# A fused attention and mixer kernel on one core: the sixth key/value chunk, the weight conversions and six channel pieces get other places in the order

## The chip, the cores and the metric

The kernel runs on one core of a Trainium2 chip. The metric is the device time of one execution in microseconds (us). The core has a matrix engine (TensorE, PE in the rows), three engines for elementwise work (VectorE or DVE, ScalarE or ACT, GpSimd or POOL) and a queue that issues transfers (SyncE, SP). Each of them works through its own list of instructions in order; semaphores tie the lists together.

## The reference

Three layers follow one another, for 4 batches of 576 positions.

- Attention with 8 heads of width 64: q and k are rotated, `softmax(q k^T / 8) v` is taken per head, and the heads are laid side by side into `x` of 512 features.
- A channel mix: `xk = mu_k*x + (1-mu_k)*x_prev` and `xr` likewise with `mu_r`, where `x_prev` is `x` moved by one position; then `v = relu(xk @ w_k)^2 @ w_v` (1024 hidden features) and `r = sigmoid(xr @ w_r)`; the output is `r * v`.
- A token and channel mixer: `u = x + (relu(x^T @ w_tok1) @ w_tok2)^T`, and `u + relu(u @ w_ch1) @ w_ch2` with 1536 hidden channels.

The weights arrive as 64-bit floats and are converted on the chip; each operand of a product is split into a high and a low part, and three products (high by high, high by low, low by high) stand for one.

## The kernel before, in words

**Attention.** The heads are worked in 16 pairs of 9 steps, 144 steps in all. A step (`a_step`, from L640) computes a tile of scores (`S_products`, L437, six matmuls into a tile of the pool `S_p`), its row maximum on DVE (L448), the exponential on ACT (L461), the sum's reciprocal on DVE (L471, L473), a high half on ACT (L78, tile `p`) and a low half on DVE (L484). Two or three transposing transfers (L565, L567) then bring the halves into the layout of the second product, `emit_pv` (L580), whose result DVE scales into `x` (`out`, L584 to L586; the rows show the helper's line L85). The last pair's last `out` is the last output of attention. `S_p` has three score tiles of two PSUM banks each, `pv_p` and `acc_p` have one bank each: eight banks in all.

**Keys and values.** `kvr_gen` (from L716) walks over eight chunks, two of 288 positions per batch, numbered 0 to 7; the sixth chunk is n = 5. Each has 4 pieces of interpolated input (`lerp_slice`), 8 blocks `kp` of 12 matmuls (L704 to L706), whose results ACT evicts twice (L769 the relu, L773 its square), and 4 blocks `vp` of 24 matmuls, which ACT evicts at L76 (`vt`). `a_step` advances this generator three times per step at a lower priority than its own work, so that the blocks fall between the score tiles. What is left after the last step is run by the loop `while not kv.done` (L994). A block takes its accumulator from `accps` (L708): the single bank of `acc_p`, or, once `second` is set (L918, after all steps), three times out of four a tile of `S_p`. All of the sixth chunk's blocks are emitted inside the steps, so they share the one bank.

**Conversions.** `Conv` (L179) turns pieces of the 64-bit weights into split parts in four stages, two pieces per `step`: stage 0 loads (L203, SP), stage 1 rescales the high words on ACT (L211), stage 2 merges the words on DVE (L218, L219, L221, and L226 for a row maximum of channel weights), stage 3 writes the high part on ACT (L76 or L78) and the low part on DVE (L107 or L239). `conv1` (L942) holds `w_r` (4 pieces), `w_tok1` (5), `w_tok2` (2) and the first six pieces of `w_ch2`; three of its steps are emitted before the loop at L994 and one with each turn of it. `conv2` (L1014) holds eight pieces of `w_ch1`, `conv3` the rest.

**Gates and tokens.** `gate_gen` (L943) makes four pieces `xs` of `xr` for each half of a batch (ACT L78, DVE L958, ACT L76, POOL L107), in a pool of four buffers that the keys also used, and then four blocks `rp` of 12 matmuls. `tok_gen` (L882 to L912) is the token mixer. Both are interleaved by a loop that also steps `conv2`; the channel mixer `ch_gen` (L1124 to L1128, `c1p` and `co`) follows with `conv3`.

**What sets the order.** A tile scheduler traces the whole program, simulates it, and lists the instructions per engine by readiness and by a priority that grows in the order of emission; `ahead(n)` moves instructions forward by n. `order` and `behind` add an edge that the simulated order must respect, without a semaphore between engines. A tile is given a buffer when one is free in that order.

Of the kernel before, what the change touches and what calls it, by code (L numbers as in the profile page):

```python
# [8 lines left out]
F32R = mybir.dt.float32r  # L9
# [3 lines left out]
ALU = mybir.AluOpType  # L13
# [3 lines left out]
B, H, S, D = 4, 8, 576, 64  # L17
NP = H // 2
QW = 640
HS = 288  # L20
# [8 lines left out]

PV_AT = {7: 0, 12: 1}  # L30

UNIT = [(0, 256), (256, 320)]

KVN, WARM = 5, (22, 4, 4)

CW, HALF, TWICE = DCH // 2, KC // 2, 3

PACE, STEP, REST = (24, 28), 1, 8

RAW, LOW = 3, "P"  # L40

# [26 lines left out]
def body(tc, kin, qin, vw, tabs, ident, mu, w_k, w_v, w_r, w_t1, w_t2, w_c1, w_c2, out):  # L68
# [18 lines left out]
    class ahead:  # L87

        def __init__(self, n):
            self.n = n  # L90
# [19 lines left out]
    with ctx:  # L110
# [11 lines left out]
        P = {}  # L122
# [51 lines left out]
        def behind(o, name):  # L174

            if name in last:
                order(o, last[name])

        class Conv:  # L179


            def __init__(self, cv, weights, name, load=None, low="P", room=None, after=None):
                self.cv, self.name, self.load, self.low, self.room, self.after = cv, name, load, low, room, after
                self.q = [(w, i) for w in weights for i in range(len(w.srcs))]
                if weights[-1].raw:
                    self.q[:0] = [None] * (len(self.q) % 2)
                self.n, self.words, self.t = 0, {}, {}
# [4 lines left out]
            def stage(self, j, i):  # L192
                if not 0 <= i < len(self.q) or self.q[i] is None:
                    return
                weights, k = self.q[i]
                src = weights.srcs[k]
                w = src.shape[1]
                wide = src.dtype == I64
                if j == 0:
                    raw = self.words[i] = weights.words(k)  # L200
                    if self.load:
                        behind(pool.memset(raw[:, 0:1], 0), self.load)
                    sp.dma_start(raw if wide else raw[:, :w], src.bitcast(I32))  # L203
                    return
                if j < 3:
                    hl = self.words[i].rearrange("p (a b) -> p a b", b=2)
                    lw, hw = hl[:, :, 0], hl[:, :, 1]
                if j == 1:
                    v = self.t[i] = self.cv()[:, :w]
                    x = hw if wide else self.words[i][:, :w]  # L210
                    o = act.activation(out=v.bitcast(F32), in_=x.bitcast(F32), func=AF.Copy,  # L211
                                       scale=REBIAS if wide else 1.0)
                    if self.after:
                        behind(o, self.after)
                elif j == 2 and wide:
                    v = self.t[i]
                    m = self.room()[:, :w] if self.room else v
                    yield lambda: dve.tensor_scalar(out=m, in0=v, scalar1=3, scalar2=None, op0=ALU.logical_shift_left)  # L218
                    yield lambda: dve.scalar_tensor_tensor(out=m, in0=hw, scalar=SIGN, in1=m, op0=ALU.bitwise_and,  # L219
                                                           op1=ALU.bitwise_or)  # L220
                    yield lambda: dve.scalar_tensor_tensor(out=v, in0=lw, scalar=29, in1=m,  # L221
                                                           op0=ALU.logical_shift_right, op1=ALU.bitwise_or)
                    if weights.raw:
                        rows, c = weights.rows
                        o = c + k if weights.cut == 1 else 2 * KD + k
                        yield lambda: dve.tensor_reduce(out=rows[:, 0, o:o + 1], in_=v.bitcast(F32),  # L226
                                                        op=ALU.max, axis=AX.X, apply_absolute_value=True)
                elif j == 3 and weights.raw:
                    rows, c = weights.rows
                    o = c + k // weights.cut  # L230
                    if i % 2 == 0 and weights.cut == 2:
                        dve.tensor_tensor(rows[:, 0, o:o + 1], rows[:, 0, 2 * KD + k:2 * KD + k + 1],
                                          rows[:, 0, 2 * KD + k + 1:2 * KD + k + 2], op=ALU.max)
                        p2(rows[:, :, o:o + 1])
                    elif i % 2 == 0:
                        p2(rows[:, :, o:o + 2])
                    dst, f = weights.take(k), self.t.pop(i).bitcast(F32)
                    copy("A", dst[:, 0], f, rows[:, 1, o:o + 1])
                    yield lambda: dve.scalar_tensor_tensor(out=dst[:, 1], in0=f, scalar=rows[:, 1, o:o + 1],  # L239
                                                           in1=dst[:, 0], op0=ALU.mult, op1=ALU.subtract)  # L240
                elif j == 3:
                    dst, f = weights.take(k), self.t.pop(i).bitcast(F32)
                    copy("A", dst[:, 0], f)
                    tt(self.low, dst[:, 1], f, dst[:, 0].bitcast(F32), ALU.subtract)
# [324 lines left out]
        @prio("pv")  # L569
        def emit_pv(g, u):  # L570

            t0, n = UNIT[u]
            ts = [pt_t.pop((g, x, u)) for x in range(2)]
            vh, vl = v16_t[g]
            p = pv_p.tile([128, 512], F32, tag="pv", name="pv")
            prods = [(vh, j, j) for j in range(9)] + [(vl, j, j) for j in range(5)]
            for i, (v, a, c) in enumerate(prods):
                for x in (1, 0):
                    l = slice(64 * x, 64 * x + 64)
                    pe.matmul(p[l, 0:n], lhsT=v[:, a, l], rhs=ts[x][:, c, :], start=(i == 0),  # L580
                              stop=(i == len(prods) - 1))

            @prio("low")
            def out():  # L584
                b, pr = divmod(g, NP)
                copy("D", x_of(b)[:, pr, 1 + t0:1 + t0 + n], p[:, 0:n], sc_t[g][:, 1:2])  # L586
                if u == 1:
                    x_done(g)
            return out
# [117 lines left out]

        def accps(nm):  # L708
            n_acc[0] += 1
            if second and n_acc[0] % 4:  # L710
                return S_p.tile([128, 2, 512], F32, tag="S", name=nm)[:, 0]
            return acc_p.tile([128, 512], F32, tag="acc", name=nm)

# [2 lines left out]
        def kvr_gen(seq, ready):  # L716
# [28 lines left out]
            for n, (kind, b, c) in enumerate(seq):  # L745
# [4 lines left out]
                if len(xs_of[n]) < KD:  # L750
                    if not xs_of[n]:
                        yield 0
                    while len(xs_of[n]) < KD:
                        lerp(n)
                        tick()
                        yield 0
                xs = xs_of[n]
                k2 = [None] * KF
                for m in range(KF):
# [98 lines left out]
            return s[1] * NP in a_done  # L858

        kv = Stream(kvr_gen([("K", b, c) for b in range(B) for c in range(2)], ready))  # L860
        second = False
        u_of, u_done, M = {}, set(), {}
        for j in range(FIRST, NTT + 5):
            a_step(j, kv.advance)
        at.close()

# [72 lines left out]
        def cv_t():  # L939
            return cv_p.tile([128, S], I32, tag="cv", name="cv")  # L940

        cv = Conv(cv_t, [wr, t1, t2, c2_part(0, HALF)], "conv1", low="D")  # L942
        def gate_gen(b):  # L943

            y = y_p[b].tile([128, KD, S], F32, tag="y", name="y")
# [3 lines left out]
            for c in range(2):  # L949
# [4 lines left out]
                for kk in range(KD):  # L954
                    a = P["a"].tile([128, HS], F32, tag="a", name="a")
                    copy("A", a, x[:, kk, o:o + HS], om_s[:, 1, kk:kk + 1])
                    f = P["f"].tile([128, HS], F32, tag="f", name="f")
                    dve.scalar_tensor_tensor(out=f, in0=x[:, kk, o + 1:o + HS + 1], scalar=mu_s[:, 1, kk:kk + 1], in1=a,  # L958
                                             op0=ALU.mult, op1=ALU.add)
                    t = P["xs"].tile([128, 2, HS], F32R, tag="xs", name="xs")  # L960
                    copy("A", t[:, 0], f)
                    tt("P", t[:, 1], f, t[:, 0].bitcast(F32), ALU.subtract)
                    xs.append(t)
                    yield 2
# [24 lines left out]

        g_done, g_up = set(), []  # L990
        gate, tok = Stream(gates()), Stream(toks())
        for _ in range(3):
            cv.step()
        while not kv.done:  # L994
            kv.advance(30)
            if len(half) == 2 * B and not g_up:
                gate.advance(9)
                g_up.append(1)
            if not cv.done():
                cv.step()  # L1000
# [10 lines left out]
        c2_b = c2_part(HALF, KC)  # L1011
        for nm, n in (("ytk", 1), ("h1", 2), ("uhl", 2), ("hs", 3), ("ht", 2), ("st", 2), ("top", 1)):
            M[nm] = top("m_" + nm, n)
        cv, cv3 = Conv(cv_t, c1_w[:1], "conv2", low="D"), Conv(cv_t, [c1_w[1], c2_b], "conv3", low="D", after="hs")  # L1014
        def all_max(m):

            p = tps("mp")
# [231 lines left out]
```

## Time and profile before

| | us |
|---|---|
| median of 3 runs | 924.8 |
| lowest and highest | 923.28, 929.65 |
| the profiled execution's own time | 928.29 |
| its span, first to last instruction | 926.5 |
| PE busy in the span | 869.4 |

The profile is one execution. Its span is 1.8 us shorter than its own time, which is 3.5 us over the median. Engines are busy at the same time, so their busy times don't add up to the span; for each stage one asks which engine has no room left, and what an idle engine was waiting for.

### The profile page before, as it was taken

The page shows a single profiled execution, that of the slowest core. Times are in us where ns is not written, and L with a number is a line of the kernel's source. Part 1 is how long each engine was busy: PE and PEld are TensorE (multiplying, and loading weights), DVE is VectorE, ACT ScalarE, POOL GpSimd, SP SyncE. Part 2 cuts the span into 40 slices and gives each one's busy share as a digit, 9 for nine tenths or more (in the row PEclk, how much of TensorE's full clock was granted, in tenths as well). Part 3 has the DMA queues.
Part 4 walks back from the last instruction along what each step waited for, and adds up shares of the span by engine and source line. Part 5 has one row for each costly group of instructions (what it writes and reads, how often), then busy time and mean ns, then how long its engine had stood idle before and what let it go on. Part 6 is the DMA issues. An engine that isn't in the chain of part 4 may idle for free.

```text
span 926.5 us, 19002 instructions
## 1 busy us (share of the span) xinstructions
PE 869.4 (94%) x7004; PEld 762.4 (82%) x7004; DVE 620.2 (67%) x1462; ACT 516.9 (56%) x1158; POOL 459.1 (50%) x512
## 2 busy tenths in 40 slices
PE   8899779989989989998899899999999999999998
PEld 5788668889878868897799799998878888888876
DVE  5789877676776757877998745455889445546332
ACT  4798677666876756966655555544456422323221
POOL 6998968776776682623633355422123222222221
PEclk9999979999999989998999999999999999999999
DMA  8786599999999969999836520001220001000000
GB/s 236 255 308 188 134 207 187 209 192 195 204 206 183 221 143 176 153 201 237 289 116 208 151 96 8 2 1 35 75 92 24 1 1 52 27 27 27 27 27 26
DMA packets 172493, 119.17 MB, mean 129 GB/s; under 512 B 133488, under 2 KB 148976, under 8 KB 171888
## 3 DMA queue, kind: packets, MB, share of 16 engines
q1 hardware_dynamic: 172400, 117.95, 52.9%
q8 instruction: 55, 0.90, 0.4%
q14 instruction: 38, 0.31, 0.1%
HBM read 60.90 MB, written 14.16 MB: 81 GB/s over the span
## 4 chain that ended last, share of the span: by engine, by line
PE 43%; DVE 6%; DMA 2%; ACT 2%; issue 2%; POOL 1%; SPq 0%; DVEq 0%; ACTq 0%; POOLq 0%
PE co L704 5%; PE c1p L704 5%; PE c1p L705 5%; PE c1p L706 5%; PE co L705 5%; PE co L706 5%; PE rp L705 2%; PE rp L704 2%; PE rp L706 2%; DVE cv L219 1%; DVE cv L221 1%; PE t2p L911 1%; PE t2p L912 1%; PE t2p L910 1%; PE trp L882 1%
## 5 line engine op out<-in xcount | busy, mean ns | idle before, releaser
L107 POOL TENSOR_TENSOR hs<-ht,hs 128x288 f16<-128x288 f32 x96 | 73.3, 764 | 229.6 <-DVE ht L1128 115.6
L437 PE MATMUL S<-kz,kq 128*128 128x288 f32 x744 | 127.5, 309 | 12.3 <-DVE p L484 3.4
L1124 ACT ACTIVATE hs<-c1p,top 128x288 f16<-128x288 f32 x96 | 47.7, 497 | 161.7 <-PE c1p L706 160.2
L448 DVE TENSOR_REDUCE nm<-S 128x1 f32<-128x576 f32 x144 | 107.9, 753 | 34.0 <-PE S L437 33.2
L437 PEld LDWEIGHTS S<-kz,kq 128*128 128x128 f32 x744 | 107.1, 193 | 23.3 <-issue 14.7
L705 PE MATMUL c1p<-uhl,parts 128*128 128x288 f16 x384 | 109.8, 286 | 0.0
L706 PE MATMUL c1p<-uhl,parts 128*128 128x288 f16 x384 | 109.7, 286 | 0.0
L704 PE MATMUL c1p<-uhl,parts 128*128 128x288 f16 x384 | 109.5, 286 | 0.0
L705 PE MATMUL co<-hs,parts 128*128 128x288 f16 x384 | 108.7, 286 | 0.0
L706 PE MATMUL co<-hs,parts 128*128 128x288 f16 x384 | 108.6, 286 | 0.0
L704 PE MATMUL co<-hs,parts 128*128 128x288 f16 x384 | 105.1, 286 | 0.3 <-ACT hs L1124 0.3
L484 DVE SCALAR_TENSOR_TENSOR p<-S,rc,p 128x576 f16<-128x576 f32 x108 | 85.9, 812 | 17.9 <-ACT p L78 17.3
L461 ACT ACTIVATE S<-S,nm 128x576 f32<-128x576 f32 x108 | 76.9, 715 | 36.5 <-DVE nm L448 36.1
L704 PEld LDWEIGHTS <-parts 128*128 128x128 f16 x768 | 75.1, 98 | 19.3 <-issue 0.5
L705 PEld LDWEIGHTS <-parts 128*128 128x128 f16 x768 | 75.2, 98 | 18.8
L706 PEld LDWEIGHTS <-parts 128*128 128x128 f16 x768 | 75.2, 98 | 18.5
L704 PE MATMUL kp<-xs,parts 128*128 128x288 f32 x256 | 79.4, 313 | 9.9 <-ACT t L769 6.9
L107 POOL TENSOR_TENSOR q<-t 128x288 f32<-128x288 f32 x64 | 45.5, 713 | 80.7 <-ACT t L769 70.7
L78 ACT ACTIVATE p<-S,rc 128x576 f16<-128x576 f32 x108 | 79.0, 754 | 10.6 <-DVE rc L473 6.2
L1128 DVE TENSOR_SCALAR ht<-c1p,top 128x288 f32<-128x288 f32 x60 | 30.9, 516 | 77.7 <-ACT hs L1124 77.7
L704 PE MATMUL vp<-k,parts 128*128 128x288 f32 x256 | 76.0, 301 | 3.5 <-ACT vt L76 1.9
L705 PE MATMUL kp<-xs,parts 128*128 128x288 f32 x256 | 77.7, 304 | 0.2 <-POOL xs L107 0.2
(154 smaller groups left out, 2392.7 us busy)
## 6 DMA issues: line engine op xcount, KB each, us to landing
rq<-in_qin_dram SPq DMA_DIRECT2D x30, 320.0 KB, 4.1
kz<-kq SPq DMA_DIRECT2D x64, 144.0 KB, 2.9
rk<-in_kin_dram SPq DMA_DIRECT2D x30, 288.0 KB, 3.8
words<-in_w_c_dram SPq DMA_DIRECT2D x12, 512.0 KB, 4.2
words<-in_w_c_dram SPq DMA_DIRECT2D x16, 384.0 KB, 3.5
vr<-in_vw_dram SPq DMA_DIRECT2D x16, 320.0 KB, 3.5
xd<-xT SPq DMA_DIRECT2D x16, 288.5 KB, 3.3
xT<-xd SPq DMA_DIRECT2D x4, 1154.0 KB, 5.8
```

The source lines that it names most:

```text
L78: act.activation(out=o, in_=i, func=AF.Copy, scale=scale)
L107: return (pool if e == "P" else dve).tensor_tensor(o, a, b, op=op)
L219: yield lambda: dve.scalar_tensor_tensor(out=m, in0=hw, scalar=SIGN, in1=m, op0=ALU.bitwise_and, op1=ALU.bitwise_or)
L437: o = pe.matmul(p[:, h, 0:HS], lhsT=a[l, 128 * m:128 * m + 128], rhs=b[l, h * HS:(h + 1) * HS], start=(n == 0), stop=(n == 2))
L448: last["max"] = dve.tensor_reduce(out=nm, in_=S_t[j][:, :, 0:HS], op=ALU.max, axis=AX.XY, negate=True)
L461: act.activation(out=e, in_=e, func=AF.Exp, bias=sum_t[j], accum_out=s)
L484: last["lo"] = dve.scalar_tensor_tensor(out=t[:, 1], in0=S_t.pop(j)[:, :, 0:HS], scalar=sum_t[j], in1=t[:, 0], op0=ALU.mult, op1=ALU.subtract)
L704: pe.matmul(p, lhsT=wh, rhs=t[:, 0], start=first, stop=False)
L705: pe.matmul(p, lhsT=wh, rhs=t[:, 1], start=False, stop=False)
L706: pe.matmul(p, lhsT=wl, rhs=t[:, 0], start=False, stop=last)
L1124: last["hs"] = act.activation(out=h[:, 0], in_=p[:, 0:HS], func=AF.Relu, scale=g)
L1128: dve.tensor_scalar(out=f, in0=p[:, 0:HS], scalar1=g, scalar2=0.0, op0=ALU.mult, op1=ALU.max)
```

## The change

Five edits.

- The sixth chunk (`HELD = 5`) is not started until the flag `wide` is set, at the last but one of the 144 steps (`LATE = 2`). A step emits the score tile of two steps later, so by then the program has emitted them all.
- From then on `accps` may take tiles of `S_p`: the test is `wide`, no longer `second`.
- Stage 1 and the first instruction of stage 2 of `conv1` are ordered behind `last["out"]`, the last output of attention; `out` names the instruction for this. The eviction itself is the same instruction as before.
- `conv1` is stepped twice ahead of the loop, no longer three times, and the loop advances the keys by 60, no longer by 30, per step of the conversions. The six pieces of `w_ch2` move from `conv1` to the end of `conv2`.
- The pieces `xs` of the second half (c = 1) of each batch take their buffers from the pool `uhl`, which the channel mixer uses later.

```diff
--- before.py
+++ after.py
@@ -29,13 +29,15 @@
 
 PV_AT = {7: 0, 12: 1}
 
+HELD, LATE = 5, 2
+
 UNIT = [(0, 256), (256, 320)]
 
 KVN, WARM = 5, (22, 4, 4)
 
 CW, HALF, TWICE = DCH // 2, KC // 2, 3
 
-PACE, STEP, REST = (24, 28), 1, 8
+PACE, STEP, REST, SPREAD = (24, 28), 1, 8, 60
 
 RAW, LOW = 3, "P"
 
@@ -179,8 +181,8 @@
         class Conv:
 
 
-            def __init__(self, cv, weights, name, load=None, low="P", room=None, after=None):
-                self.cv, self.name, self.load, self.low, self.room, self.after = cv, name, load, low, room, after
+            def __init__(self, cv, weights, name, load=None, low="P", room=None, after=None, then=None):
+                self.cv, self.name, self.load, self.low, self.room, self.after, self.then = cv, name, load, low, room, after, then
                 self.q = [(w, i) for w in weights for i in range(len(w.srcs))]
                 if weights[-1].raw:
                     self.q[:0] = [None] * (len(self.q) % 2)
@@ -210,12 +212,15 @@
                     x = hw if wide else self.words[i][:, :w]
                     o = act.activation(out=v.bitcast(F32), in_=x.bitcast(F32), func=AF.Copy,
                                        scale=REBIAS if wide else 1.0)
-                    if self.after:
-                        behind(o, self.after)
+                    for x in (self.after, self.then):
+                        behind(o, x)
                 elif j == 2 and wide:
                     v = self.t[i]
                     m = self.room()[:, :w] if self.room else v
-                    yield lambda: dve.tensor_scalar(out=m, in0=v, scalar1=3, scalar2=None, op0=ALU.logical_shift_left)
+                    o = dve.tensor_scalar(out=m, in0=v, scalar1=3, scalar2=None, op0=ALU.logical_shift_left)
+                    if self.then:
+                        behind(o, self.then)
+                    yield
                     yield lambda: dve.scalar_tensor_tensor(out=m, in0=hw, scalar=SIGN, in1=m, op0=ALU.bitwise_and,
                                                            op1=ALU.bitwise_or)
                     yield lambda: dve.scalar_tensor_tensor(out=v, in0=lw, scalar=29, in1=m,
@@ -583,7 +588,8 @@
             @prio("low")
             def out():
                 b, pr = divmod(g, NP)
-                copy("D", x_of(b)[:, pr, 1 + t0:1 + t0 + n], p[:, 0:n], sc_t[g][:, 1:2])
+                last["out"] = dve.tensor_scalar(out=x_of(b)[:, pr, 1 + t0:1 + t0 + n], in0=p[:, 0:n],
+                                                scalar1=sc_t[g][:, 1:2], scalar2=None, op0=ALU.mult)
                 if u == 1:
                     x_done(g)
             return out
@@ -707,7 +713,7 @@
 
         def accps(nm):
             n_acc[0] += 1
-            if second and n_acc[0] % 4:
+            if wide and n_acc[0] % 4:
                 return S_p.tile([128, 2, 512], F32, tag="S", name=nm)[:, 0]
             return acc_p.tile([128, 512], F32, tag="acc", name=nm)
 
@@ -754,6 +760,9 @@
                         lerp(n)
                         tick()
                         yield 0
+                while n == HELD and not wide:
+                    tick()
+                    yield 0
                 xs = xs_of[n]
                 k2 = [None] * KF
                 for m in range(KF):
@@ -858,9 +867,10 @@
             return s[1] * NP in a_done
 
         kv = Stream(kvr_gen([("K", b, c) for b in range(B) for c in range(2)], ready))
-        second = False
+        second = wide = False
         u_of, u_done, M = {}, set(), {}
         for j in range(FIRST, NTT + 5):
+            wide = j >= NTT - LATE
             a_step(j, kv.advance)
         at.close()
 
@@ -939,7 +949,8 @@
         def cv_t():
             return cv_p.tile([128, S], I32, tag="cv", name="cv")
 
-        cv = Conv(cv_t, [wr, t1, t2, c2_part(0, HALF)], "conv1", low="D")
+        c2_a = c2_part(0, HALF)
+        cv = Conv(cv_t, [wr, t1, t2], "conv1", low="D", then="out")
         def gate_gen(b):
 
             y = y_p[b].tile([128, KD, S], F32, tag="y", name="y")
@@ -957,7 +968,12 @@
                     f = P["f"].tile([128, HS], F32, tag="f", name="f")
                     dve.scalar_tensor_tensor(out=f, in0=x[:, kk, o + 1:o + HS + 1], scalar=mu_s[:, 1, kk:kk + 1], in1=a,
                                              op0=ALU.mult, op1=ALU.add)
-                    t = P["xs"].tile([128, 2, HS], F32R, tag="xs", name="xs")
+                    if c == 0:
+                        t = P["xs"].tile([128, 2, HS], F32R, tag="xs", name="xs")
+                    else:
+                        if kk % 2 == 0:
+                            two = M["uhl"].tile([128, 2, 2, HS], F32R, tag="uhl", name="xs")
+                        t = two[:, kk % 2]
                     copy("A", t[:, 0], f)
                     tt("P", t[:, 1], f, t[:, 0].bitcast(F32), ALU.subtract)
                     xs.append(t)
@@ -989,10 +1005,10 @@
 
         g_done, g_up = set(), []
         gate, tok = Stream(gates()), Stream(toks())
-        for _ in range(3):
+        for _ in range(2):
             cv.step()
         while not kv.done:
-            kv.advance(30)
+            kv.advance(SPREAD)
             if len(half) == 2 * B and not g_up:
                 gate.advance(9)
                 g_up.append(1)
@@ -1011,7 +1027,7 @@
         c2_b = c2_part(HALF, KC)
         for nm, n in (("ytk", 1), ("h1", 2), ("uhl", 2), ("hs", 3), ("ht", 2), ("st", 2), ("top", 1)):
             M[nm] = top("m_" + nm, n)
-        cv, cv3 = Conv(cv_t, c1_w[:1], "conv2", low="D"), Conv(cv_t, [c1_w[1], c2_b], "conv3", low="D", after="hs")
+        cv, cv3 = Conv(cv_t, [c1_w[0], c2_a], "conv2", low="D"), Conv(cv_t, [c1_w[1], c2_b], "conv3", low="D", after="hs")
         def all_max(m):
 
             p = tps("mp")
```

## Rows read from the trace of the kernel before

**Rows 1.** The page, busy time and share of the span of each engine.
```profile
PE 869.4 (94%) x7004; PEld 762.4 (82%) x7004; DVE 620.2 (67%) x1462; ACT 516.9 (56%) x1158; POOL 459.1 (50%) x512
```
**Rows 2.** Busy time by stretch; the first of the rows names the columns.
```profile
core 0: us, PE busy (x) PEld busy (x) DVE busy (x) ACT busy (x) POOL busy (x), PEclk, DMA share, GB/s
361.70:413.20 51.50, 49.47 (x414) 46.20 (x413) 39.53 (x95) 38.76 (x88) 21.99 (x29) 1.00 0.93 179
413.20:429.40 16.20, 16.10 (x146) 15.12 (x145) 11.37 (x26) 10.40 (x24) 4.39 (x6) 1.00 0.99 196
...
432.40:442.70 10.30, 8.58 (x34) 7.54 (x32) 10.02 (x18) 6.19 (x14) 4.54 (x6) 0.50 1.00 194
...
477.50:516.50 39.00, 38.37 (x288) 37.91 (x286) 33.23 (x72) 22.89 (x55) 14.02 (x17) 1.00 0.55 176
516.50:534.70 18.20, 14.38 (x97) 12.98 (x96) 13.11 (x31) 10.60 (x25) 8.00 (x9) 1.00 0.48 145
534.70:612.00 77.30, 77.27 (x608) 76.94 (x609) 39.52 (x89) 40.69 (x110) 38.03 (x48) 1.00 0.07 26
612.00:700.00 88.00, 86.13 (x699) 72.87 (x698) 63.77 (x170) 43.59 (x102) 21.32 (x26) 1.00 0.17 54
```
**Rows 3.** Groups of PE, 429.4 to 445.2: count | busy us, mean ns | idle before, releaser.
```profile
L704 PE MATMUL kp<-xs,parts 128*128 128x288 f32 x19 | 7.3, 401 | 4.2 <-ACT t L769 4.2
```
**Rows 4.** Timeline, 424 to 441, all engines: start, us, engine, line, [idle before].
```profile
427.19 9.10 SPq L567 DMA_TRANSPOSE pt<-p  x3
...
430.11 0.66 ACT L211 ACTIVATE cv<-words 128x512 f32<-128x512 f32 x1 [3.20 <-DMA words<-in_w_r_dram]
...
430.88 0.43 DVE L218 TENSOR_SCALAR cv<-cv 128x512 int32<-128x512 int32 x1 [2.84 <-ACT cv L211]
...
431.75 0.40 PE L704 MATMUL kp<-xs,parts 128*128 128x288 f32 x1 [2.36 <-ACT t L769]
...
432.67 0.75 DVE L448 TENSOR_REDUCE nm<-S 128x1 f32<-128x576 f32 x1
```
**Rows 5.** Groups of PE, 445.2 to 461.5.
```profile
L704 PE MATMUL vp<-k,parts 128*128 128x288 f32 x17 | 5.3, 313 | 0.9 <-ACT vt L76 0.7 <-ACT t L769 0.2
...
L704 PE MATMUL kp<-xs,parts 128*128 128x288 f32 x9 | 2.4, 307 | 1.3 <-ACT xs L76 1.3
```
**Rows 6.** Timeline, the last product of attention on PE and its output on DVE.
```profile
449.00 0.85 PE L580 MATMUL pv<-pt,vl 128*64 128x320 f16 x10
...
453.67 0.54 DVE L85 TENSOR_SCALAR xT<-pv,sc 128x320 f32<-128x320 f32 x1
```
**Rows 7.** Groups of PE, 461.5 to 516.5.
```profile
L704 PE MATMUL kp<-xs,parts 128*128 128x288 f32 x52 | 15.7, 301 | 1.8 <-ACT vt L76 1.2 <-ACT t L769 0.6
```
**Rows 8.** Groups of PE, 516.5 to 534.7, the first gate blocks.
```profile
L705 PE MATMUL rp<-xs,parts 128*128 128x288 f32 x32 | 9.6, 309 | 1.5 <-POOL xs L107 1.4
...
L704 PE MATMUL rp<-xs,parts 128*128 128x288 f32 x32 | 7.7, 301 | 2.2 <-ACT vt L76 1.7 <-ACT xs L76 0.6
```
**Rows 9.** Groups of PE, 413.2 to 429.4, the last scores.
```profile
L704 PE MATMUL kp<-xs,parts 128*128 128x288 f32 x16 | 4.9, 308 | 0.0
```
**Rows 10.** Groups of DVE, 445 to 490: channel pieces (512 wide) in conversion.
```profile
L219 DVE SCALAR_TENSOR_TENSOR cv<-words,cv 128x512 int32<-128x512 int32 x6 | 4.6, 761 | 0.0
L221 DVE SCALAR_TENSOR_TENSOR cv<-words,cv 128x512 int32<-128x512 int32 x6 | 4.5, 758 | 0.0
...
L226 DVE TENSOR_REDUCE rows<-cv 128x1 f32<-128x512 f32 x6 | 4.0, 673 | 0.0
...
L239 DVE SCALAR_TENSOR_TENSOR parts<-cv,rows,parts 128x512 f16<-128x512 f32 x4 | 3.1, 787 | 0.4 <-ACT parts L78 0.4
L218 DVE TENSOR_SCALAR cv<-cv 128x512 int32<-128x512 int32 x6 | 3.0, 497 | 0.0
```
**Rows 11.** Groups of ACT, 445 to 490: the same pieces.
```profile
L211 ACT ACTIVATE cv<-words 128x512 f32<-128x512 f32 x6 | 3.9, 665 | 0.2 <-DVE parts L239 0.2
...
L78 ACT ACTIVATE parts<-cv,rows 128x512 f16<-128x512 f32 x4 | 2.7, 716 | 1.7 <-DVE rows L134 1.7
```

## The prediction

> **What bounds the kernel now.** The page comes first: TensorE is busy 869.4 us, 94% of the span, and no other engine over 67% [rows 1]. No edit takes a matmul away, so the change can win only where TensorE idles, or works at its lower clock, and can lose only by making new such places. The busy time by stretch says where these are [rows 2]. From 361.7 to 413.2 TensorE idles 2.0 of 51.5 us and in the last scores, 413.2 to 429.4, it idles 0.1 of 16.2. Behind them it does badly: from 432.4 to 442.7 the granted clock is 0.50, the lower of its two levels. In the gates, 516.5 to 534.7, it is busy 14.4 of 18.2 us; from 534.7 to 612 it idles nowhere. So the change is about 429 to 535, and I went through that stretch by groups of instructions and by timeline.
>
> Right behind the last scores, the blocks of the sixth chunk lose 4.2 us waiting for ACT's eviction of the block before [rows 3], as they share one bank. The first and longest of these waits has a cause of its own: ACT had a conversion in front, which stood 3.20 us for its words from memory; DVE stood 2.84 us behind it, and the last row maximum, whose scores the stretch to 429.4 holds [rows 2], began at 432.67 [rows 4]. TensorE idled 2.36 us and its clock fell soon after. Attention's last product ended at 449.85, its output on DVE began only at 453.67, among conversions [rows 6], and the seventh chunk's blocks then waited 1.3 us for their last input piece [rows 5].
>
> **The change part by part.** I sum against the profiled execution, 928.3 us, and go over to the median, 3.5 us lower, at the end. A matmul at the full clock takes 38.37 us / 288 = 0.133 us, by the stretch from 477.5 [rows 2].
>
> *Chunk held.* Between 413.2 and 429.4, 48 of its matmuls ran (three lines of 16 [rows 9]), 48 x 0.133 = 6.4 us of TensorE. They go behind the scores. The scores can end earlier by what then binds them: TensorE would have 16.1 - 6.4 = 9.7 us left, DVE has 11.4, ACT 10.4 with the chunk's evictions in it [rows 2]. A score tile passes through DVE, ACT, DVE, ACT, DVE before its buffer is free, so I don't expect DVE to be packed: I take 12.8 us for this stretch in place of 16.2, so 3.4 us of the 6.4 come back. Cost 3.0 us; the ends are 1.6 (DVE packed, 16.2 - 11.4 = 4.8 back) and 6.4 (no earlier end of the scores). If the one block in four that keeps its own bank slips in among the scores, 12 x 0.133 = 1.6 us less, so nought at best.
>
> *Accumulators in score tiles.* With the score tiles free one after another, a block need not wait for the eviction before it. Of the 4.2 us [rows 3] I take 3.2 back; 1.0 stays because the first tiles come free only when the last low halves are made. Ends 1.0 and 4.2.
>
> *The clock.* From 432.4 to 442.7, 34 matmuls took 8.58 us, where 34 x 0.133 = 4.5 would do: 4.1 us lost [rows 2]. The fall stands behind the idle 2.36 us [rows 4]. With that wait gone I take 3.0 us back, not 4.1, since TensorE will have shorter gaps among the last scores and the transposes of the last probabilities must still land. Ends: 0 and 4.1. This is the term that I know least.
>
> *Conversions behind the last output.* What they delay goes: the wait of ACT and DVE in front of the last tile (its price for TensorE is in the terms above), and the output's wait of 453.67 - 449.85 = 3.8 us [rows 6], with which the 1.3 us for the late piece goes, and some of the other 0.9 [rows 5]. I take 1.9 back, ends 0 and 2.2. What is late next is the transposes: three of the last tiles' sat 9.10 us in SP's queue behind four loads of weights [rows 4]. Those loads are stage 0, which the new edge does not hold, so this stays, and it is why I don't let the output come more than the 3.8 us and the earlier scores allow. The added edge is one of order, not a wait: nothing queues behind it on ACT; on DVE the output simply stands in front. `w_r` is wanted only at 518, some 65 us of key work after, so later conversions hide.
>
> *Six pieces moved, steps half as dense.* From 461.5 to 516.5 TensorE idles 1.8 us for ACT evictions [rows 7]; ACT and DVE had the conversions in their lists there. Thinner conversions give perhaps 0.7 back (ends 0 and 1.8). The six pieces go to the gates and tokens. A piece costs DVE 0.50 + 0.76 + 0.76 + 0.67 + 0.79 = 3.48 us [rows 10], six 20.9, and ACT 6 x (0.665 + 0.716) = 8.3 [rows 10, 11]. In the stretch 534.7 to 612 DVE is busy 39.5 of 77.3 and ACT 40.7 [rows 2]: there is room, 37.8 and 36.6 us, and the pieces are wanted only by the channel mixer at its end. The nearest like case is 612 to 700, where conversions run beside channel products, DVE is busy 63.8 of 88, and TensorE keeps 86.1 [rows 2]. I take a cost of 0.5 for places where a conversion stands in front of a token operation; ends 0 and 3.
>
> *Gate pieces in other buffers.* The second half's blocks wait 1.4 + 0.6 = 2.0 us for their pieces [rows 8], which wait in turn for buffers that the first half's blocks still read. With buffers of their own the pieces can be made ahead. I take 1.5 back, ends 0 and 2.0: the buffers lie where key tiles lay, which may come free late. The 1.7 us for `vt` at the first gate block [rows 8] is the change of PSUM pools and stays.
>
> Sum: -3.0 + 3.2 + 3.0 + 1.9 + 0.7 - 0.5 + 1.5 = 6.8 us saved. 928.3 - 6.8 = 921.5 for a run like the profiled one, and 3.5 lower on the median: **918.0 us**, 0.7% under 924.8.
>
> **The rivals.** All are on the median.
>
> *All of it comes back.* Every wait goes and the clock holds: -1.6 + 4.2 + 4.1 + 2.2 + 1.8 - 0 + 2.0 = 12.7, which gives 912.1. For it: each of these has one named cause that the edits touch. Against it: seven places at their best at once.
>
> *The clock falls anyway, and earlier.* Without the chunk the scores leave TensorE some 9.7 us of work in up to 16.2, in pieces; if the clock falls among them, the scores end no sooner (cost 6.4), and the chunk starts at the lower level, so nothing of the 4.1 returns: -6.4 + 3.2 + 0 + 1.9 + 0.7 - 0.5 + 1.5 = 0.4, or 924.4. For it: one idle of 2.36 us was enough to be followed by the fall at 432.4 [rows 2, 4]. Against it: the gaps among the scores should be about 1 us each. The Trainium skill (TensorE: Matmul & The Clock Gate, "What's actually happening") speaks for this rival: there the throttled state is the default and only recent activity lifts it. The trace agrees that idle comes first (2.36 us idle, then 0.50); what shorter gaps do, no row here says.
>
> *Slower: conversions stand in front of the tokens.* One mechanism, in the gate and token stage: DVE's list is in order, and each merge put in front of a token subtraction holds the transposes and products that follow it. The price is the share s of 20.9 us that TensorE waits. The other terms give 7.3, so it decides from s = 7.3 / 20.9 = 0.35; at s = 0.6 it costs 12.5, and the time is 924.8 + 12.5 - 7.3 = 930. For it: TensorE is at its bound there, so any wait shows. Against it: 612 to 700 [rows 2].
>
> *The change doesn't do what it says.* The scheduler may find the old bank or order as early in its simulation, or the held chunk may be listed behind the seventh's inputs; then the gaps change places and the time is 924.8 within 2.
>
> **How the numbers follow.** Forecast with its own range of 914 to 922: 0.45. All comes back: 0.22. Clock falls: 0.20. Conversions in front: 0.08. No effect: 0.05. A measurement of this kernel can tell about 1% from no change, so 915.6 and 934.0 are the marks. Faster by more takes most of the second case (0.20), and a quarter of the first (0.12): 0.32. Slower by more takes the far part of the fourth and what I haven't thought of: 0.07. The rest is 0.61. The range 910 to 927 leaves out the far end of the second case and most of the fourth, some 0.15.
>
> **What would show it.** In the changed profile: no `kp` of the sixth chunk in the main run of the last scores, or one block at most; the last score some 3 us earlier, about 426; blocks behind it with waits of about 1 us for ACT in place of 4.2; the last output under 1 us behind its product, with no conversion in front of it on ACT or DVE; no wait for `xs` in the second gate half; channel conversions between 530 and 600 with TensorE still full. The forecast is wrong if the granted clock is 0.50 for some 10 us around the last scores, if the scores end at 429 or later, or if TensorE idles over 3 us between 535 and 612.

## The result and the profile after

The changed kernel takes 915.58 us (median of 4 runs, 914.55 to 916.43) where the kernel before takes 924.04; the ratio is 0.9896, with a 95% interval of 0.9854 to 0.9938, so 5.7 to 13.5 us were saved. The forecast was 918.0 us, in a range of 910 to 927. The profiled execution of the changed kernel took 916.43 us, its span 914.6.

The two profiles differ by 11.9 us of span, and not all of that is the change. The first rows say why. They are the matmuls of the tile `vp` (last line of its three products), first in a window that ends with the fourth chunk, then over the whole span; of `rp`; and of the score tiles without `kz` (count: duration ns min/median/max, first and last start). Of the kernel before:

```profile
L706 PE MATMUL vp<-k,parts x32: 292/295/445, 329.9 to 359.3; 128*128 128x288 f32 x32
...
L706 PE MATMUL vp<-k,parts x256: 291/295/445, 159.9 to 516.2; 128*128 128x288 f32 x128
...
L706 PE MATMUL rp<-xs,parts x128: 291/297/302, 518.5 to 615.5; 128*128 128x288 f32 x128
...
L437 PE MATMUL S<-kq x120: 286/295/442, 8.4 to 429.1; 128*128 128x288 f32 x96, 64*128 64x288 f32 x24
```

The same of the changed kernel:

```profile
L712 PE MATMUL vp<-k,parts x32: 291/295/308, 325.8 to 353.3; 128*128 128x288 f32 x32
...
L712 PE MATMUL vp<-k,parts x256: 289/295/402, 159.1 to 500.2; 128*128 128x288 f32 x128
...
L712 PE MATMUL rp<-xs,parts x128: 291/297/302, 501.3 to 603.7; 128*128 128x288 f32 x128
...
L442 PE MATMUL S<-kq x120: 286/294/442, 8.8 to 420.8; 128*128 128x288 f32 x96, 64*128 64x288 f32 x24
```

Up to the end of the fourth chunk (359.3 and 353.3) the engines' lists are the same in both kernels, so these 6.0 us are not the change. From there on I cut every profile at four marks, the last starts in such rows: A, the end of the fourth chunk; B, the last score; C, the last key block; D, the last gate block; E is the end of the span.

| | A to B | B to C (keys) | C to D (gates, tokens) | D to E | A to E |
|---|---|---|---|---|---|
| before | 69.8 | 87.1 | 99.3 | 311.0 | 567.2 |
| changed | 67.5 | 79.4 | 103.5 | 310.9 | 561.3 |
| difference | -2.3 | -7.7 | +4.2 | -0.1 | -5.9 |

So by the traces the change saves 5.9 us, at the lower end of what the runs gave: 10.0 up to the last key block, of which the gates and tokens give 4.2 back. Profiles of e6 and e9 below, whose four engines work through the same lists as the changed kernel's, give 6.1 and 6.5. The stretches of the changed kernel, with the columns of [rows 2]:

```profile
410.20:421.10 10.90, 9.00 (x93) 8.14 (x92) 7.33 (x18) 6.63 (x14) 0.00 (x0) 1.00 1.03 207
421.10:447.80 26.70, 26.35 (x210) 25.70 (x211) 15.17 (x30) 14.78 (x33) 18.24 (x21) 1.00 1.05 300
447.80:500.50 52.70, 51.83 (x384) 50.82 (x383) 42.11 (x91) 32.74 (x81) 18.77 (x22) 1.00 0.46 152
500.50:514.00 13.50, 13.05 (x96) 12.82 (x96) 11.30 (x22) 7.83 (x17) 6.87 (x8) 1.00 0.63 206
514.00:604.00 90.00, 84.20 (x638) 81.25 (x639) 62.49 (x137) 48.79 (x129) 44.34 (x51) 1.00 0.16 53
```

The lower clock of [rows 2] is gone: 1.00 throughout. TensorE idles 0.35 us in the 26.7 behind the last score, where [rows 3] had 4.2 in 15.8. The first gate takes 13.5 us in place of 18.2. But from 514 to 604 TensorE idles 5.8 us, and DVE is busy 62.49 us; the kernel before had this in the matching stretch, with the same 638 matmuls:

```profile
534.70:615.80 81.10, 81.07 (x638) 80.74 (x639) 40.38 (x91) 42.28 (x114) 40.41 (x51) 1.00 0.07 25
```

What TensorE waits for there, in the changed kernel (the chart of waits: total us, times, longest):

```profile
PE rp L710 <- ACT xs L78: 2.1, 3, 1.1
PE rp L710 <- DVE y L109: 1.0, 1, 1.0
PE t1p L906 <- DVE ytk L109: 0.9, 3, 0.5
PE trp L892 <- ACT q L985: 0.8, 1, 0.8
```

None of these existed before in the matching stretch. DVE's own list tells what stands in front (timeline of DVE, 512 to 524):

```profile
511.92 1.15 DVE L224 SCALAR_TENSOR_TENSOR cv<-words,cv 128x384 int32<-128x384 int32 x2
512.99 1.15 DVE L226 SCALAR_TENSOR_TENSOR cv<-words,cv 128x384 int32<-128x384 int32 x2
514.06 0.51 DVE L969 SCALAR_TENSOR_TENSOR f<-xT,mu_s,a 128x288 f32<-128x288 f32 x1
514.49 1.14 DVE L231 TENSOR_REDUCE rows<-cv 128x1 f32<-128x384 f32 x2
```

A gate piece (L969) sits between merges of a conversion, and TensorE's first block of the second batch waits for it. ACT stood 3.52 us for that piece (timeline of ACT, 514.5 to 522). The conversions' part on ACT stands in the way too: ACT writes two high parts (`parts`) ahead of the `q` that `trp` waits for.

```profile
514.60 0.44 ACT L78 ACTIVATE xs<-f 128x288 fp32r<-128x288 f32 x1 [3.52 <-DVE f L969]
...
517.83 1.11 ACT L80 ACTIVATE parts<-cv,rows 128x384 f16<-128x384 f32 x2
518.84 0.39 ACT L985 ACTIVATE q<-rp 128x288 f32<-128x288 f32 x1
```

### The profile page after: what moved, and what is told of

Read it like the earlier page. It is cut to its first block, busy times and chain, and to the rows that moved or that the text cites. A ratio compares the mean times of both kernels' runs of the same rounds, so it can differ in the third digit from the quotient of the medians.

```text
span 914.6 us, 18987 instructions
## 1 busy us (share of the span) xinstructions
PE 860.7 (94%) x7004; PEld 756.3 (83%) x7004; DVE 619.1 (68%) x1468; ACT 514.3 (56%) x1155; POOL 456.2 (50%) x506
## 4 chain that ended last, share of the span: by engine, by line
PE 44%; DVE 5%; DMA 4%; issue 2%; ACT 2%; POOL 1%; SPq 0%; DVEq 0%; ACTq 0%; POOLq 0%
PE co L710 5%; PE c1p L710 5%; PE c1p L711 5%; PE c1p L712 5%; PE co L711 5%; PE co L712 5%; DMA vd<-vt 1%; DMA pt<-p 1%; DMA y<-vd 1%; PE kp L710 1%; PE kp L712 1%; PE kp L711 1%; PE rp L710 1%; PE rp L712 1%; PE rp L711 1%
## 5 line engine op out<-in xcount | busy, mean ns | idle before, releaser
L80 ACT ACTIVATE p<-S,rc 128x576 f16<-128x576 f32 x108 | 79.2, 754 | 11.9 <-DVE rc L478 5.0
L710 PE MATMUL kp<-xs,parts 128*128 128x288 f32 x256 | 77.5, 304 | 5.0 <-ACT t L778 2.6
L710 PE MATMUL vp<-k,parts 128*128 128x288 f32 x256 | 75.5, 299 | 2.9 <-ACT t L778 1.6
L711 PE MATMUL vp<-k,parts 128*128 128x288 f32 x256 | 75.6, 297 | 2.3 <-POOL k L109 2.3
```

Source lines behind the costliest of these rows:

```text
L80: act.activation(out=o, in_=i, func=AF.Copy, scale=scale)
L710: pe.matmul(p, lhsT=wh, rhs=t[:, 0], start=first, stop=False)
L711: pe.matmul(p, lhsT=wh, rhs=t[:, 1], start=False, stop=False)
```

## The experiments

Theory A: the held chunk, its accumulators and the edge behind the last output carry the gain in the keys; conversions that now lie among gates and tokens stretch that stage. Rival B: the gates and tokens are bound by a chain of their own, so that time saved ahead of them is given back. The totals of single kernels move by over 1% from run to run, so the marks decide. This table holds all kernels that follow; the ratio is to the kernel before.

| | A to B | B to C | C to D | A to E | ratio, 95% interval |
|---|---|---|---|---|---|
| before | 69.8 | 87.1 | 99.3 | 567.2 | |
| changed | 67.5 | 79.4 | 103.5 | 561.3 | 0.9896 (0.9854, 0.9938) |
| e1 pieces back | 68.8 | 82.0 | 101.6 | 563.4 | 0.9956 (0.9919, 0.9992) |
| e2 old gate buffers | 66.3 | 79.4 | 108.1 | 564.8 | 0.9954 (0.9924, 0.9984) |
| e3 no edge | 66.9 | 85.3 | 103.5 | 566.7 | 0.9986 (0.9943, 1.0028) |
| e4 no hold | 69.8 | 81.5 | 103.6 | 565.9 | 0.9993 (0.9955, 1.0031) |
| e5 pieces first | 66.5 | 82.0 | 102.3 | 561.8 | 0.9897 (0.9855, 0.9939) |
| e6 denser steps | 66.7 | 79.8 | 103.6 | 561.1 | 0.9891 (0.9842, 0.994) |
| e7 e6 and e1 | 67.3 | 82.3 | 102.7 | 563.3 | 0.9941 (0.9896, 0.9986) |
| e8 gate buffers alone | 70.2 | 87.4 | 97.8 | 566.4 | 0.9921 (0.9889, 0.9953) |
| e9 low priority | 67.2 | 78.9 | 103.6 | 560.7 | 0.9924 (0.9888, 0.996) |
| e10 no pieces | 67.1 | 83.5 | 96.5 | 558.1 | one run |
| e11 no conv2 | 67.0 | 83.9 | 96.5 | 558.8 | one run |
| e12 one bank | 69.0 | 81.7 | 103.6 | 565.3 | 0.9991 (0.9945, 1.0036) |

**e1, the six pieces back in conv1.**

```diff
-        cv = Conv(cv_t, [wr, t1, t2], "conv1", low="D", then="out")
+        cv = Conv(cv_t, [wr, t1, t2, c2_a], "conv1", low="D", then="out")
...
-        cv, cv3 = Conv(cv_t, [c1_w[0], c2_a], "conv2", low="D"), ...
+        cv, cv3 = Conv(cv_t, c1_w[:1], "conv2", low="D"), ...
```

> The changed kernel with the six channel pieces back at the end of conv1, all other edits kept. Changed kernel: 915.6 us; from its last key block (500.4) to its last gate block (604.0) 103.5 us pass, against 99.3 before. Theory A, the pieces stand in the lists of DVE and ACT in front of gate and token operations: that stage shrinks to 95 to 98 us, the keys lose 1 to 2 us to ACT evictions, and the time is 909 to 912 us. Rival B, the gates are bound by their own chain of pieces and loads, so that time saved ahead of them is given back whatever the conversions do: the stage stays at 101 to 105 us and the time at 914 to 918 us.

The stage went to 101.6 us, into B's range; A's 95 to 98 failed, and the keys lost 2.6 where A had 1 to 2. The traces show a reason other than B's chain: the `w_ch1` pieces, now behind the channel pieces, moved into the gates in their place. Seven of their merges, 384 wide (L226), lie in the stage, where the changed kernel and the kernel before have three. What holds the stage, e1 can't decide; e10 does. A to B is 1.3 us longer because the clock fell there (see the clock rival below).

**e2, the gate pieces of the second half in the old buffers.** The branch on `c` in `gate_gen` is taken out again.

> The changed kernel with the second half's gate pieces back in the four buffers of the first half. Theory A: the first gate's second half waits again for its pieces, about 2 us at the first batch and little after it, 917 to 920 us. Rival C, the new buffers let pieces be made in an order that holds up the token work and so cost the later batches what they give the first: 910 to 914 us. Rival B, whatever the first batch gains is given back anyway: 915 to 917 us.

The gate stage grows by 4.6 us, to 108.1, and A to E by 3.5, as A had it; rivals B and C fall. In the first gate the old wait is back:

```profile
L710 PE MATMUL rp<-xs,parts 128*128 128x288 f32 x32 | 8.3, 324 | 2.7 <-ACT xs L78 2.2 <-ACT vt L78 0.5
```

But the 4.6 us are not waiting alone. The granted clock fell twice in these gates, to 0.50 from 514.9 to 518.3 and from 525.1 to 528.5. From the first to the last gate block TensorE is busy 3.3 us longer than in the changed kernel, for the same matmuls, and idles only 1.2 us more. What the buffers are worth at the full clock, e2 doesn't show.

**e3, no edge behind the last output.**

```diff
-        cv = Conv(cv_t, [wr, t1, t2], "conv1", low="D", then="out")
+        cv = Conv(cv_t, [wr, t1, t2], "conv1", low="D")
```

> The changed kernel without the edge that puts conv1 behind attention's last output. Theory A: conversions stand again in front of the last score tile and of the last output, the last output slips from about 436 us by 3 us or more, and the sixth and seventh chunk wait: 917 to 921 us. Rival D, the held chunk has work enough to cover that tail: the output slips, no block waits, 915 to 917 us.

The keys lose 5.9 us, and the last output slips to 444.7, from 436.3 in the changed kernel. Rival D falls. And the gates take 103.5 us as in the changed kernel, though the keys end later: B would have had them shorter.

**e4, the chunk not held.** `HELD = 5` becomes `HELD = -1`.

> The changed kernel with the sixth chunk not held, so that it is emitted among the steps again and shares the one bank; all else kept. Theory A, the hold and the score tiles as accumulators carry the gain of the keys: the waits for ACT and the lower clock behind the scores come back, 6 to 8 us, 921 to 924 us. Rival E, the first wait came from a conversion in front of the eviction, which the kept edge removes, and the clock fell for that wait alone: only 1 to 3 us come back, 916 to 918.5 us, with the granted clock at its upper level.

A to C is 4.4 us longer. Both had something: waits for ACT come back, but only 2.5 us of them, and in the keys the clock does not fall. These are the group of `kp` from the last score to the last key block, and that stretch with the columns of [rows 2]:

```profile
L710 PE MATMUL kp<-xs,parts 128*128 128x288 f32 x80 | 23.4, 304 | 2.8 <-ACT t L778 2.5 <-ACT vt L78 0.3
```
```profile
428.70:510.20 81.50, 76.37 (x557) 72.48 (x556) 55.06 (x113) 45.80 (x109) 36.25 (x43) 1.00 0.59 185
```

**e12, the chunk held but in the one bank.** In `accps`, `wide` becomes `second` again.

> The changed kernel with the sixth chunk still held, but its accumulators from the one bank as before (score tiles only after all steps). Theory A, the score tiles carry a part of the gain of their own: the chunk's blocks wait 0.5 to 0.6 us each for ACT again, 3 to 5 us over eight blocks, the keys from the last score go from 79.4 to 82 to 85 us, and the time is 918 to 921 us in a like run. Rival H, once no conversion stands in front of ACT the eviction is fast enough: 79 to 81 us, 915 to 917 us.

A to C is 3.8 us longer, so the score tiles as accumulators carry a part of the gain, but not by A's mechanism. These are the waits from the last score to the last key block (groups of TensorE):

```profile
L711 PE MATMUL kp<-xs,parts 128*128 128x288 f32 x88 | 26.0, 297 | 1.0 <-DVE xs L109 1.0
L710 PE MATMUL kp<-xs,parts 128*128 128x288 f32 x88 | 25.9, 301 | 1.0 <-ACT t L778 0.6 <-ACT xs L78 0.4
...
L585 PE MATMUL pv<-pt,vh 128*64 128x320 f16 x18 | 1.4, 302 | 2.1 <-DMA pt<-p 2.1
```

The blocks wait 0.6 us in all for ACT's eviction, where A had 0.5 to 0.6 each: there H was right. The larger waits are for the last transposes (2.1 us), which the one-bank order put in TensorE's way, and for input pieces (1.4). The keys took 81.7 us, between the two ranges; A to E is 4.0 us longer, in A's range.

**e5 to e7, where the conversions go.** e5 has `[c2_a, c1_w[0]]` in conv2, e6 `SPREAD = 30`, e7 that and the edit of e1.

> The changed kernel with the six channel pieces ahead of the eight w_ch1 pieces in conv2. The first of the w_ch1 pieces was finished only when the last key product had freed its place (489.2 us, 1.5 us behind the seventh chunk's successor's last key block), and DVE had room before that. Theory A, what runs of conversions inside the gate stage is what stretches it: the channel pieces move ahead of the end of the keys, and the stage from the last key block to the last gate block goes from 103.5 to 99 to 101 us; the keys lose 0 to 2 us; 912 to 915 us in a like run. Rival B, the gates' own chain: the stage stays at 102 to 105 us.

> The changed kernel with a conversion step after every 30 units of key work in place of 60, the channel pieces still in conv2. Theory A: conv1 ends sooner, but the w_ch1 pieces still wait for their place and the channel pieces stand behind them, so the stage stays at 102 to 104 us; the keys lose up to 2 us to denser conversions. Rival F, it is the thinner steps that push conversions into the gates: the stage falls to 97 to 99 us.

> The changed kernel with a conversion step after every 30 units and the channel pieces back in conv1: the hold, the edge, the score tiles and the gate buffers alone are left of the change. Theory A: conversions end within 25 us of the last key block as before, so the stage is 94.5 to 97 us (99.3 before less the 4.5 that the gate buffers gave); the keys, from the last score to the last key block, go from 79.4 to 81 to 84 us; the time is 4 to 6 us under the changed kernel in a like run. Rival B: the stage stays over 100 us.

e6 is the changed kernel over again, with the same lists on every engine: the density of the steps does nothing, rival F falls. e5 and e7 take 1.2 and 0.8 us off the gates and put 2.6 and 2.9 on the keys, like e1; both times the stage stays in B's range and A's number fails, for e7 (94.5 to 97) by 6. With the keys 5 us shorter than before, the same row of conversions reaches into the gates whichever piece comes last: in both, as in e1, seven merges of `w_ch1` lie there in place of three. The clock fell in these gates too (0.50 from 529.0 to 532.4 in e5, from 523.4 to 530.2 in e7), so neither gives a clean price.

**e8, the gate buffers alone, on the kernel before.**

> The kernel before with only the second half's gate pieces in the buffers of uhl. Theory A: the keys take 87 us as before, the first gate 13.5 to 15 us in place of 18.1, the stage from the last key block to the last gate block 94.5 to 96 in place of 99.3, and the time is 4 us under the kernel before. Rival B: what the first gate gains is given back in the later ones, the stage stays at 98 to 100 us and the time is the same.

The stage shrinks by 1.5 us only, to 97.8, between the two. Here the wait behind the scores and the lower clock are there as before (timeline of TensorE; the stretch behind it):

```profile
425.57 0.40 PE L704 MATMUL kp<-xs,parts 128*128 128x288 f32 x1 [2.50 <-ACT t L769]
```
```profile
426.40:433.30 6.90, 5.20 (x21) 4.51 (x20) 6.63 (x13) 3.95 (x10) 3.04 (x4) 0.51 1.17 167
```

The runs gained more than the trace: a ratio of 0.9921 (0.9889 to 0.9953) is over 4 us, where A to E is 0.8 us shorter. Up to A the lists are those of the kernel before, so what lies behind the rest stays open. The same may hold for a part of what the runs gave the changed kernel.

**e9, conv2 at a lower priority** (`conv2=-300` in `PRI`).

> The changed kernel with conv2 at a lower priority (300 places later), so that gate and token operations are listed ahead of its instructions where both are ready; the channel pieces ended 60 us behind the last key block, 44 us before the last gate block, so there is room. Theory A, conversions in front of gate and token operations stretch the stage: 103.5 us fall to 98 to 101, 911 to 914 us in a like run. Rival G, the scheduler lists them by readiness and the engines meet another order than it simulated, so a priority moves little: 102.5 to 104 us, no change.

No change in the stage, as rival G had it. The lists of TensorE, DVE, ACT and GpSimd are the same as in the changed kernel: the priority moved nothing, so e9 does not test what conversions in front would cost.

**e10 and e11, the conversions left out.** In e10 `c2_a` is set by `pool.memset`, its row maxima to 1; in e11 the first half of `w_ch1` too, and `conv2` does nothing.

> The changed kernel with the conversion of the first six channel pieces left out (they are set to nought by GpSimd, their row maxima to one). Theory A: the stage from the last key block to the last gate block falls from 103.5 to 98 to 100 us. Rival B, the gates' own chain: 102 us or more.

> The changed kernel with all of conv2 left out (the first half of w_ch1 and the six channel pieces are set to nought, their row maxima to one), so that the gate stage holds no conversion. Theory A: the stage falls to 94 to 96 us, what its matmuls take, and the first gate stays at 13 to 13.6. Rival B: over 99 us, as the gates then wait for their own pieces and loads.

Both take 96.5 us, well under B's figures, and just beside A's: e10 1.5 below them, e11 0.5 above. So the six pieces cost 103.5 - 96.5 = 7.0 us in the gates, and the few `w_ch1` pieces at their beginning nothing. The stretch behind the first gate, and its waits, in e10:

```profile
521.60:604.60 83.00, 82.02 (x638) 81.00 (x639) 42.91 (x95) 43.16 (x118) 41.29 (x51) 1.00 0.06 22
```
```profile
PE rp L710 <- ACT xs L78: 0.7, 2, 0.4
PE rp L711 <- POOL xs L109: 0.3, 1, 0.3
```

DVE is busy 19.6 us less than in the changed kernel and TensorE idles 1.0 in place of 5.8. How much of the 7.0 us is due to DVE's part of the conversions and how much to ACT's was not tried. The keys of both are 4 us longer than in the changed kernel; GpSimd sets the pieces in that time and the clock falls once, and which part of the 4 us is whose was not tried. Rival B is out: e3, e4 and e12 end the keys at three different lengths and take 103.5 to 103.6 us for the gates, and e10 takes 96.5. Nor does TensorE set the length at their beginning: in the gates of e4, e6 and e9 the clock fell to 0.50 for 3.4 us, and the stage took 103.6 us all the same.

## Why the prediction was right, and where it was not

The time lay in the range and its sign was right, but two terms were wrong and nearly cancelled: the forecast of the sum was 6.8 us, the traces give 5.9, made up of 10.0 and -4.2 where I had 5.8 and +1.0. (The medians of the runs give 8.5.) That the total came out is in part luck.

*Chunk held.* Right. One block of the chunk ran among the last scores, as allowed for, so 36 matmuls or 4.8 us were moved, and the last score came 2.3 us earlier (forecast: 6.4 and 3.4). Cost 2.5, against 3.0. In the eight kernels that have the same matmuls up to there and kept the clock, A to B is 66.3 to 67.3, so the cost is 2.5 or up to 1.2 less.

*Accumulators, clock, conversions behind the output, denser keys.* I took 3.2 + 3.0 + 1.9 + 0.7 = 8.8 back. The keys are 7.7 us shorter with 4.8 us more work in them, so 12.5 came back, and the upper ends of the four add to 4.2 + 4.1 + 2.2 + 1.8 = 12.3. In the keys the rival that all comes back was the right one in its total, though not in its parts. I had shaded each term as if they were independent; they hung on one another. The conversion in front of ACT made the long wait, and behind the long wait the clock fell: in the three kernels without the edge (before, e8, e3) the clock fell behind the last score, each time behind one wait of 2.25 to 2.50 us; in e4, with the edge and without the hold, it held through the keys. Of e3, the wait and the stretch behind it:

```profile
438.50 0.40 PE L710 MATMUL vp<-k,parts 128*128 128x288 f32 x1 [2.25 <-ACT t L778]
```
```profile
439.50:442.90 3.40, 3.40 (x17) 3.40 (x16) 3.40 (x8) 0.73 (x2) 2.87 (x4) 0.50 1.06 360
```

Edge, hold and score tiles are worth 5.3, 4.4 and 3.8 us up to the last key block (e3, e4, e12 against the changed kernel). Together that is more than the 10.0 won: they overlap. And two of the terms were not what I had priced. With the edge and the hold in place the one bank costs 0.6 us of waits for ACT (e12), not 3.2. The thinner steps give nothing (e6); what came back in the later keys goes with taking the six pieces out of them (e1 puts them back and loses 2.6 us there).

*The output.* Right: last product ended at 436.30, output from 436.34 (timeline of DVE):

```profile
436.34 0.55 DVE L591 TENSOR_SCALAR xT<-pv,sc 128x320 f32<-128x320 f32 x1 [0.92 <-PE pv L585]
```

The transposes stayed as slow as I had said, 9.03 us for three, and nothing waited for them. The edge binds the simulated order alone: on the chip ACT began its first conversions at 434.81, 1.5 us ahead of the output, which they did not hold up.

*Six pieces moved.* This is the step that failed: that DVE's idle time in the gates and tokens would hide the conversions. I priced them at 0.5 us with ends of 0 and 3, because DVE had 37.8 us of room in the stage and a like stretch later kept TensorE full. The work was sized rightly (20.9 us on DVE, 19.6 measured). Its price was 7.0 us (e10), a share of 7.0 / 20.9 = 0.33 of it: the mechanism of my slower rival, whose deciding share was 0.35. One of my own signs of being wrong came with it: TensorE idles 5.8 us in the stretch where I had allowed 3. Nor is it the move alone. Back in their old place the pieces relieve the gates by only 1.9 and 0.8 us (e1, e7), as `w_ch1` comes in their stead; I had taken it for granted that "later conversions hide". Room on average was the wrong measure. A gate piece passes ACT, DVE, ACT, GpSimd, the first two through single buffers, and a token tile passes ACT and DVE between two sets of matmuls; a conversion in front of one of them holds that chain. That the channel mixer from 612 on is no like case, because its products don't hang on DVE in such short turns, is my reading of the program and not tested.

*Gate buffers.* I took 1.5. Alone they are worth 1.5 us (e8); in the changed kernel 4.6 (e2), a part of which goes with the lower clock there.

*The clock rival* did not come in the profiled execution: gaps among the last scores of 1.40 and 0.44 us, granted clock 1.00. It came in e1, whose list is the same there: a wait of 1.91 us for the transposes, then 0.51 from 414.6 to 418.0, and A to B 1.3 us longer. The Trainium skill (TensorE: Matmul & The Clock Gate, "What's actually happening") ties the throttled state to recent idleness. The traces agree that idleness comes first; they don't give one length of wait that decides, as the last section shows.

## What to carry to other kernels

Price work that is moved into a stage by the chains it will stand in, not by the idle share of the engine: here about 40 us of spare time on DVE (83.0 less 42.9 in e10) did not hide 20 us of conversions. And where several losses follow from one wait, forecast them together: here, when the wait went, all went. A profile pair is compared from the last point up to which the instruction lists are the same.

## What the runs showed that I had not expected

The same lists of instructions, up to the end of the fourth chunk, took 352.2 to 359.3 us over the fourteen profiles, a spread larger than the change is worth by the traces; the kernel before gave single times as far apart as 915.7 and 930.2 us. A part of the spread may go with the clock, whose mean up to A is 0.96 in the kernel before and 0.98 in the changed one; not all of it, as e7 has 0.96 too and reached A at 353.3.

The clock fell behind quite different idles. Behind 2.25 to 2.50 us it fell each time, and behind 1.80 and 1.76 in the keys of e10 and e11 too; behind 2.11 us in e12 it did not; and in the gates of e4, e6 and e9 it fell where no single wait was over 1.2 us (in e6 at 518.0). The changed kernel, e3 and e12 have the same waits for `xs` in the gates (1.10 and 0.76 us in the changed kernel) and kept their clock. Both stretches of e6, before the fall and in it:

```profile
518.00:521.50 3.50, 3.46 (x16) 3.14 (x15) 3.44 (x9) 3.31 (x10) 2.34 (x3) 0.51 0.01 2
513.00:518.00 5.00, 2.81 (x18) 2.19 (x19) 3.75 (x10) 3.86 (x11) 3.43 (x5) 1.00 0.59 219
```

There TensorE was busy 2.81 of 5.00 us ahead of the fall; in the like stretch of the changed kernel (514.5 to 519.5) it was busy 2.89 of 5.00, and no fall came. The fall cost the stage nothing: it takes 103.6 us in the three kernels with it and 103.5 to 103.6 in the three without.
